# Modulation vectors and a column sum by fp32r matmuls, relu of phi(k) on ScalarE, and three moved groups of instructions, in a linear-attention and token-mixer block

## The chip, the cores and the metric

The kernel runs on one core of one Trainium2 chip. The metric is the time of one execution in device microseconds, lower is better. Three runs of the kernel before the change gave a median of 456.86 us.

## The reference

The input x has 2048 tokens of 448 channels. A conditioning vector c gives six modulation vectors of 448 numbers each. Two residual blocks follow: linear attention with 16 heads of 28 channels, and an MLP that mixes along the token axis with 1792 hidden units. All is float32.

```python
mod = silu(c) @ w_mod                       # (1,448) @ (448, 6*448): sa, ca, ga, sb, cb, gb
h = layernorm(x) * (1 + ca) + sa
q, k, v = heads(h @ wqkv)
phi = lambda t: where(t > 0, t + 1, exp(t)) + 1e-6
kv, z = phi(k)^T v, sum over tokens of phi(k)          # per head
o = (phi(q) kv) / (phi(q) z + 1e-6)
x = x + ga * (o @ wo)
h = layernorm(layernorm(x) * (1 + cb) + sb)
x = x + gb * ((gelu(h^T w1 + b1)) w2 + b2)^T
```

## The kernel before

**Numbers in two parts.** Most products run as fp32r matmuls. A float32 tile is cut into a high part (a ScalarE copy with an fp32r output) and a low part (VectorE subtracts the high part from the whole); `split` does both, lines 74 and 75. A product then takes three matmuls: high by high, high by low, low by high. A few matmuls are plain fp32; the trace shows each of those as two matmul instructions.

**Order.** The order on every engine is the order of the calls in the source: the scheduler is in its manual mode. Buffers come from pools. A tile of the pool `slots` (76 buffers) waits until the last readers of the buffer that it is given are done, so a new tile in the middle changes which buffer each later tile is given, and so what its writer waits for. PSUM has 8 banks.

**Stage one (up to 124 us).** x comes in 16 tiles of 128 tokens. For tile t VectorE makes the moments (`a_stats`, with a power on GpSimd, line 272) and the modulated norm (`a_norm_a`, `a_norm_b`, lines 277 and 283); ScalarE copies 64 columns of h once more (`a_dup`, line 287); TensorE transposes h (line 295); `a_split` cuts the transpose; `project` (11 matmuls, line 316) makes k. phi(k) is made by `a_exp` (line 323: exp on ScalarE) and `phi_k` (line 327: min with 1 and plus 1e-6 on VectorE; line 328: max of k in PSUM with 0, plus the former). `a_pk_parts` cuts phi(k): high part on ScalarE, low part either on VectorE (tiles in `DVE_LOW`) or by ScalarE's negated copy and an accumulating DMA that GpSimd issues (lines 357 and 358). A second accumulating DMA adds phi(k) to one of two running sums (line 383). `a_outer` (line 398, 11 matmuls) adds the outer product of phi(k) and h three steps later. The loop over t at line 514 takes these in an interleaved order; q of most tiles is left for later (`late`).

After the loop the running sums are summed over the tokens by two fp32 matmuls with a matrix of ones (`zp`, lines 574 to 576), `a_outer` of tile 15 follows, and the result is copied to `zb`. The outer products go through the value weights (`kvb`, line 598), a head mask, and wo (`wp`, line 723).

**Modulation vectors.** For vector j, four tiles of w_mod (112 by 448) are scaled by silu(c) and added on VectorE: `mod_acc` at one place (lines 156, 158) or `mod_part` one tile at a time (lines 164, 166). `mod_sum` (line 173) sums over the partitions by an fp32 matmul with ones, `mod_out` copies to SBUF. Vectors 1 and 0 are made at the very start, 2 inside the loop, 4 and 3 after it, 5 in stage two.

**Stage two (124 to 216 us).** A loop over i (line 731) takes, per round, the transposes of the normalized phi(q) (`tq`, line 642), the product with wo (`op`, line 658), a q projection while any is left, and from the fifth round the first MLP matmuls (`up`, lines 709 to 711) of tile i-5. VectorE's list per round is written out at lines 756 to 789; in it `b_recip`, `b_low2` (line 706, the low part of the normed tile, which waits for ScalarE's high part) and `b_scale` (line 631, `pn`, which the next round's `tq` reads) stand in this order.

**Stage three (216 us to the end)** is the rest of the MLP: w1 and w2 come in pieces, are cut and multiplied; part of the products of w2 use a scheme with seven products of halves.

Of the kernel before, what the change touches and what calls it, by code (L numbers as in the profile page):

```python
# [14 lines left out]
P = 128  # L15
# [3 lines left out]
G = 112  # L19
# [8 lines left out]
DVE_LOW = (0, 1, 13, 14, 15)  # L28
AHEAD = 8
LAG = 5  # L30
QS = {0: 2, 4: 2}
WARM = 12
WARM2, WARM3 = 10, 5
# [9 lines left out]
def block_kernel(ctx: ExitStack, tc: tile.TileContext, x, wqkv, wo, w1, b1, w2, b2, c, wmod, out):  # L43
# [16 lines left out]
    def slot(name, w=D, dt=F32, parts=P):  # L60
        return slots.tile([parts, w], dt, name=name, tag="slot", padded_shape=[P, 512])
# [5 lines left out]
    def moving(new, name, dt=F32R, parts=P):  # L67
        return new(name, dt=dt, parts=parts, w=512)[:, 16:16 + D]

    def bank(name):  # L70
        return psum.tile([P, 512], F32, name=name, tag="bank")
# [5 lines left out]

    ones = cst.tile([P, P], F32, name="ones")
    nc.vector.memset(ones, 1.0)
    ident = cst.tile([P, P], F32, name="ident")  # L80
    make_identity(nc, ident)
    mask = cst.tile([G, D], F32, name="mask")
# [78 lines left out]
    def mod_part(j, k):  # L161
        if k == 0:
            macc[j] = (tslot if j == 5 else slot)(f"acc{j}", parts=G)
            nc.vector.tensor_scalar_mul(macc[j], wm[j, 0], sc[:, 0:1])
        else:
            nc.vector.scalar_tensor_tensor(macc[j], wm[j, k], sc[:, k:k + 1], macc[j], op0=ALU.mult, op1=ALU.add)

    def mod_sum(j, n=4):
        ps = bank(f"modp{j}")
        todo = [(scb[:, (k - 2) * P:(k - 1) * P], wm[j, k]) for k in range(n, 4)]  # L170
        todo.insert(1, (ones[:G, :], macc.pop(j)))
        for k, (a, b) in enumerate(todo):
            nc.tensor.matmul(ps[:, :D], a, b, start=(k == 0), stop=(k == len(todo) - 1))
        return ps

    Whi, Wlo = {}, {}
# [13 lines left out]
    def w_low_dma(j, ch):  # L190
        w, r = Whi[j, ch], raw_w[j, ch]
        if ch < 3:
            Wlo[j, ch] = moving(tslot, f"wl{j}_{ch}")
            lo, hi = Wlo[j, ch], w
        else:
            lo = hi = w[64:128]
            r = r[64:128]
        nc.scalar.activation(lo, hi.bitcast(F32), AF.Copy, scale=-1.0)
        nc.gpsimd.dma_start(lo, r, accum_op=ALU.add)
# [119 lines left out]
    eks = {}  # L319

    def a_exp(t, ps):
        eks[t] = slot(f"ek{t}")
        nc.scalar.activation(eks[t], ps, AF.Exp)

    def phi_k(t, ps, new):
        dst, e = new(f"pk{t}"), eks.pop(t)
        nc.vector.tensor_scalar(e, e, 1.0, 1e-6, op0=ALU.min, op1=ALU.add)
        nc.vector.scalar_tensor_tensor(dst, ps, 0.0, e, op0=ALU.max, op1=ALU.add)
        return dst

    def phi_q(ps, name):
# [21 lines left out]
    def low(t, lo, full, hi):  # L353
        if t in DVE_LOW:
            nc.vector.tensor_sub(lo, full, hi.bitcast(F32))
        else:
            nc.scalar.activation(lo, hi.bitcast(F32), AF.Copy, scale=-1.0)
            nc.gpsimd.dma_start(lo, full, accum_op=ALU.add)
# [14 lines left out]
    def a_pk_parts(t):  # L373
        pk = pkf.pop(t)
        hi, lo = moving(slot, f"pkh{t}"), moving(slot, f"pkl{t}")
        nc.scalar.activation(hi, pk, AF.Copy)
        low(t, lo, pk, hi)
        if t in (0, 1, NT - 1):
            pksum.append(pk)
        elif t == NT - 2:  # L380
            pksum14.append(pk)
        else:
            nc.gpsimd.dma_start(pksum[t % 2], pk, accum_op=ALU.add)
        pks[t] = (hi, lo)
# [4 lines left out]
    def a_outer(t):  # L389
        if not cacc:  # L390
            cacc.extend(bank(f"cacc{ch}") for ch in range(4))
        xh, xl = xss.pop(t)
        kh, kl = pks.pop(t)
        for ch in range(4):
            s = slice(ch * P, (ch + 1) * P)
            todo = [(xh, kh), (xh, kl)] + ([(xl, kh)] if ch < 3 else [])
            for i, (a, b) in enumerate(todo):
                nc.tensor.matmul(cacc[ch][:, :D], a[:, s], b, start=(t == 0 and i == 0),  # L398
                                 stop=(t == NT - 1 and i == len(todo) - 1))
# [73 lines left out]
    a_exp(0, kp0)  # L473
    w_low_dma(0, 0)
    a_norm_b(2)
    w_low_dma(0, 1)
    a_stats(3)
    a_dup(2)
    a_pk(0, kp0)
# [34 lines left out]
    for t in range(3, NT):  # L514
        kp = project(t, 1, "kp")
        if t + 1 < NT:
            a_transpose(t + 1)
        a_outer(t - KV_LAG)
        if t in Q_EARLY:
            a_q(t)  # L520
        if t == 10:
            mp = mod_sum(2)
        if t + 1 < NT:
            a_split(t + 1)
        if t + 2 < NT:
            a_norm_a(t + 2)
        a_exp(t, kp)
        if t + 2 < NT:
            a_norm_b(t + 2)
        a_pk(t, kp)  # L530
        a_phi_q()
        a_pk_parts(t - 1)
        if t + 3 < NT:
            a_stats(t + 3)
        if t + 2 < NT:
            a_dup(t + 2)
        if t == 3:
            a_high(4)
        if t + 2 < NT:
            a_high(t + 2)  # L540
        if t == 10:
            mod_out(2, mp)
        if t + 4 < NT:
            load_x(t + 4)
        if 5 <= t < 9:
            mod_part(2, t - 5)
        if t in (10, 11):
            load_mod(14 - t)
        if t == 4:
            for g in range(4):  # L550
                w = tslot(f"wo{g}", parts=G)
                nc.sync.dma_start(w, wo[g * G:(g + 1) * G, :])
                wo_sb.append(w)
            load_qkv(2, tslot)
            b1c = cst.tile([P, NF], F32, name="b1c")
            nc.sync.dma_start(b1c, b1.rearrange("(k p) -> p k", p=P))
            b2c = cst.tile([P, NT], F32, name="b2c")
            nc.sync.dma_start(b2c, b2.rearrange("(k p) -> p k", p=P))
        if 11 <= t < 15:
            nc.vector.tensor_mul(wo_sb[t - 11], wo_sb[t - 11], mods[2][:G])  # L560
        load_to(PRE_LOAD.get(t, 0))
# [4 lines left out]
    a_phi_q()  # L566
    a_outer(NT - 3)
    a_outer(NT - 2)
    split_to(2)
    nc.vector.tensor_add(pksum[2], pksum[2], pksum14[0])  # L570
    nc.vector.tensor_add(pksum[2], pksum[2], pksum[1])
    a_q(late.pop(0))
    mod_acc(4)
    zp = bank("zp")
    for i, pk in enumerate((pksum[0], pksum[2])):
        nc.tensor.matmul(zp[:, :D], ones, pk, start=(i == 0), stop=(i == 1))
    a_outer(NT - 1)
    load_to(14)
    split_to(4)
    zb = tslot("zb")  # L580
    nc.scalar.activation(zb, zp[:, :D], AF.Copy)
    csum = []
    for ch in range(4):
        csum.append(slot(f"cs{ch}"))
# [4 lines left out]
    a_phi_q()  # L589
    a_q(late.pop(0))  # L590
    split_to(6)
    mp = mod_sum(4)
    mod_acc(3)
    kvb = bank("kvb")
    for ch in range(4):
        for g in range(4):
# [4 lines left out]
    kvm = slot("kvm", parts=G)  # L601
    nc.vector.tensor_mul(kvm, kvb[:G, :D], mask)
    mod_out(4, mp)
    mp = mod_sum(3)
    load_to(PRE + MID + 3)
    split_to(8)
    Wph, Wpl = [], []
# [18 lines left out]
    def b_recip(t):  # L626
        nc.vector.reciprocal(dens[t], dens[t])
# [103 lines left out]
    for i in range(NT + LAG):  # L731
        if i == NT - 4:
            load_mod(5)
        if NT - 3 <= i <= NT:
            mod_part(5, i - NT + 3)
        if i < NT:
            b_transpose(i)
        if 0 <= i - 1 < NT:
            b_out(i - 1)
        nq = min(len(late), QS.get(i, 1))  # L740
        for _ in range(nq):
            a_q(late.pop(0))
        t = i - LAG
        mp = mod_sum(5) if i == NT else None
        if t >= 0:
            if t == 0:
                accs = [bank(f"up{f}") for f in range(4)]
            if i > NT:
                if not early:
                    early = [bank(f"up{W1G[1][0] + f}") for f in range(W1G[1][1])]  # L750
                r = i - NT - 1
                step(NT + r, early, H2h[r], H2l[r], r == 0, False)
            step(t, accs, H2h[t], H2l[t], t == 0, t == NT - 1)
        if mp is not None:
            mod_out(5, mp)
        if i < NT:
            b_high(i)
        scale, res, norm1, norm2 = i + 1 < NT, 0 <= i - 2 < NT, 0 <= i - 3 < NT, 0 <= i - 4 < NT
        if res:
            b_res(i - 2)  # L760
        if scale:
            b_prod(i + 1)
        if norm2:
            b_norm2(i - 4, i)
        if res:
            b_mean1(i - 2, i)
        if norm1:
            b_norm1_a(i - 3)
        if scale:
            b_sum(i + 1)  # L770
        if norm1:
            b_norm1_b(i - 3, i)
        if scale:
            b_eps(i + 1)
        if i < NT:
            b_low(i)
        if norm1:
            b_mean2(i - 3, i)
        if scale:
            b_recip(i + 1)  # L780
        if norm2:
            b_low2(i - 4)
        if scale:
            b_scale(i + 1)
        a_phi_q(nq)
        load_to(14 + (i + 1) // 2)
        split_to(10 + (i + 1) // 2)
        if res or norm1:
            b_rstd(i, 0 if res else 1, 2 if norm1 else 1)
# [277 lines left out]
```

## Time and profile before

| | us |
|---|---|
| median of three runs (456.37 to 457.12) | 456.86 |
| the profiled execution | 457.06 |
| its span, first to last instruction | 455.3 |
| TensorE busy in the span | 448.9 |
| VectorE busy | 356.6 |
| ScalarE busy | 241.7 |
| GpSimd busy | 91.6 |

The profiled execution took 457.06 us, of which 455.3 lie between its first and its last instruction; 1.76 us lie around it. TensorE is granted its full clock throughout. A busy time of matmuls overlaps itself, since they are pipelined, so the cost of a matmul is read from the start of one to the start of the next.

### The profile page before, as it was taken

How to read it: one execution, taken by the hardware profiler on the slowest of the kernel's cores; microseconds unless marked ns; L12 is line 12 of the kernel's file. 1: busy time of each engine (PE TensorE's matmuls, PEld its weight loads, DVE VectorE, ACT ScalarE, POOL GpSimd, SP SyncE). 2: the span in 40 equal slices, each digit the busy share in tenths (PEclk: the TensorE clock that was granted, in tenths of full speed). 3: DMA queues.
4: the chain of work that ended last, by engine and by line, in shares of the span. 5: the costliest groups of instructions: out<-in, count | busy, mean ns of one | idle time of the engine just before them, and what ended most of it. 6: DMA issues, size and time to landing. Idle time of an engine off the chain costs nothing.

```text
span 455.3 us, 7265 instructions
## 1 busy us (share of the span) xinstructions
PE 448.9 (99%) x2378; PEld 409.9 (90%) x2378; DVE 356.6 (78%) x781; ACT 241.7 (53%) x538; POOL 91.6 (20%) x163
## 2 busy tenths in 40 slices
PE   8999999999999999999999999999999999999996
PEld 7589998988799999988999999999999999999995
DVE  4798897887899798896559676639696977798982
ACT  1649766644466576676675445236546262535350
POOL 2124676620014355554300000000000000000000
PEclk9999999999999999999999999999999999999999
DMA  7979999994200003322307553317960583528312
GB/s 220 283 186 168 170 175 225 229 219 141 71 1 2 23 24 88 74 50 48 116 22 228 171 187 113 115 40 235 281 185 23 186 231 120 170 96 254 112 57 97
DMA packets 60550, 61.85 MB, mean 136 GB/s; under 512 B 9248, under 2 KB 53856, under 8 KB 60512
## 3 DMA queue, kind: packets, MB, share of 16 engines
q1 hardware_dynamic: 54752, 52.45, 38.5%
q0 software_dynamic: 5760, 8.95, 12.0%
q8 instruction: 18, 0.29, 0.3%
q14 instruction: 20, 0.16, 0.1%
HBM read 45.09 MB, written 7.34 MB: 115 GB/s over the span
## 4 chain that ended last, share of the span: by engine, by line
PE 80%; POOL 4%; ACT 4%; DVE 4%; DMA 3%; issue 3%; SPq 1%; POOLq 0%; DVEq 0%
PE y L894 11%; PE up L711 8%; PE up L710 8%; PE up L709 8%; PE qp L316 7%; PE y L895 6%; PE cacc L398 5%; PE kp L316 5%; PE yp L709 4%; PE yp L711 4%; PE yp L710 4%; PE op L658 4%; DMA pkl<-pk 2%; DMA wm<-in_w_mod_dram 1%; ACT y L700 1%
## 5 line engine op out<-in xcount | busy, mean ns | idle before, releaser
L711 PE MATMUL up<-h2h,pl 128*128 128x448 f32 x224 | 81.3, 363 | 0.0
L710 PE MATMUL up<-h2l,ph 128*128 128x448 f32 x224 | 81.2, 362 | 0.0
L709 PE MATMUL up<-h2h,ph 128*128 128x448 f32 x224 | 81.1, 362 | 0.0
L75 DVE TENSOR_TENSOR pl<-pr,ph 128x512 fp32r<-128x512 f32 (+1 forms) x60 | 36.4, 616 | 12.3 <-ACT ph L74 7.9
L710 PEld LDWEIGHTS up<-h2l,ph 128*128 128x128 f32 x224 | 42.1, 188 | 3.3 <-issue 0.2
L709 PEld LDWEIGHTS up<-h2h,ph 128*128 128x128 f32 x224 | 41.9, 187 | 3.1 <-issue 0.2
L711 PEld LDWEIGHTS up<-h2h,pl 128*128 128x128 f32 x224 | 42.0, 188 | 2.4
L74 ACT ACTIVATE ph<-pr 128x512 fp32r<-128x512 f32 (+1 forms) x60 | 32.8, 567 | 15.9 <-PE up L710 11.1
L900 ACT ACTIVATE cc<-y 128x448 f32<-128x448 f32 x15 | 8.2, 546 | 55.4 <-PE y L895 38.6
L709 PE MATMUL yp<-uw,qw 128*128 128x448 f32 x84 | 31.2, 371 | 0.0
L710 PE MATMUL yp<-uw,qw 128*128 128x448 f32 x84 | 30.6, 365 | 0.0
L711 PE MATMUL yp<-uw,qw 128*128 128x448 f32 x84 | 30.6, 365 | 0.0
L398 PE MATMUL cacc<-pkh,xh 128*128 128x448 f32 x64 | 24.6, 385 | 0.0
L658 PE MATMUL op<-wph,pth 112*128 112x448 f32 x64 | 24.5, 383 | 0.0
L74 ACT ACTIVATE qw<-q 128x256 fp32r<-128x256 f32 (+1 forms) x56 | 18.9, 353 | 9.0 <-DMA q<-in_B_w_dram 8.5
L398 PE MATMUL cacc<-pkl,xh 128*128 128x448 f32 x64 | 23.3, 363 | 0.2 <-DMA pkl<-pk 0.2
L658 PE MATMUL op<-wph,ptl 112*128 112x448 f32 x64 | 23.2, 362 | 0.0
L658 PE MATMUL op<-wpl,pth 112*128 112x448 f32 x64 | 23.2, 362 | 0.0
L316 PE MATMUL kp<-wh,hh 128*128 128x448 f32 x60 | 22.0, 371 | 0.0
L316 PE MATMUL qp<-wh,hh 128*128 128x448 f32 x60 | 21.9, 371 | 0.0
L75 DVE TENSOR_TENSOR qw<-q,qw 128x256 fp32r<-128x256 f32 (+1 forms) x56 | 18.9, 352 | 3.8 <-ACT qw L74 3.8
L316 PE MATMUL kp<-wh,hl 128*128 128x448 f32 x60 | 21.7, 366 | 0.1
(198 smaller groups left out, 1221.0 us busy)
## 6 DMA issues: line engine op xcount, KB each, us to landing
pr<-in_B_w_dram SPq DMA_DIRECT2D x48, 256.0 KB, 3.0
a<-in_B_w_dram SPq DMA_DIRECT2D x20, 256.0 KB, 5.0
wm<-in_w_mod_dram SPq DMA_DIRECT2D x24, 196.0 KB, 5.0
a<-in_B_w_dram SPq DMA_DIRECT2D x20, 192.0 KB, 4.9
x<-in_A_x_dram SPq DMA_DIRECT2D x16, 224.0 KB, 4.6
xpark<-x SPq DMA_DIRECT2D x16, 224.0 KB, 1.9
q<-in_B_w_dram SPq DMA_DIRECT2D x28, 128.0 KB, 3.3
xb<-xpark SPq DMA_DIRECT2D x16, 224.0 KB, 4.1
```

Source lines behind the costliest of these rows:

```text
L74: nc.scalar.activation(hi, full, AF.Copy)
L75: nc.vector.tensor_sub(lo, full, hi.bitcast(F32))
L316: nc.tensor.matmul(o, a[:, ch * P:(ch + 1) * P], b, start=(n == 0), stop=(n == 10))
L398: nc.tensor.matmul(cacc[ch][:, :D], a[:, s], b, start=(t == 0 and i == 0), stop=(t == NT - 1 and i == len(todo) - 1))
L658: nc.tensor.matmul(opb[t][:, :D], a[:, s], b, start=(n == 0), stop=(n == 11))
L700: nc.scalar.activation(ys[t], ys[t], AF.Identity, bias=nb, scale=rs)
L709: nc.tensor.matmul(ps[:, :D], hi[:, sl], mh, start=first, stop=False)
L710: nc.tensor.matmul(ps[:, :D], hi[:, sl], ml, start=False, stop=False)
L711: nc.tensor.matmul(ps[:, :D], lo[:, sl], mh, start=False, stop=last)
L894: nc.tensor.matmul(ps[:, :D], h[:, s], w, start=opens and r == 0, stop=False, skip_group_check=True)
L895: nc.tensor.matmul(ps[:, :HD], l[:, s], w[:, :HD], start=False, stop=closes and r == PAIRS - 1, skip_group_check=True)
L900: nc.scalar.activation(cop[q, name], acc2[q, k][:, :D], AF.Copy)
```

## The change

1. A copy of the ones in fp32r, `ones_r`, is made on ScalarE at the start.
2. Modulation vectors 2, 3, 4 and 5: the accumulated tile is cut (`mod_split`: one ScalarE copy, one VectorE subtraction) and summed by two fp32r matmuls (`mod_sum2`) instead of one fp32 matmul. Vectors 1 and 0 stay.
3. The sum of phi(k): VectorE adds the second running sum to the first, the result is cut, and two fp32r matmuls replace two fp32 ones; they stand behind `a_outer` of tile 15 instead of ahead of it. The share of 1e-6 comes in as a bias of 2048 times 1e-6 in the copy to `zb`.
4. phi(k): ScalarE makes relu(k) beside exp(k), and VectorE takes one instruction instead of two. The 1e-6 moves into the bias of the high part's copy and into the low part's instruction.
5. The scaled additions for vectors 4 and 3 leave their two blocks of four behind the loop; they stand in steps 11 to 15 of the loop and just behind it.
6. The low part of one q weight tile moves from ScalarE and an accumulating DMA to VectorE.
7. In stage two `b_scale` stands ahead of `b_low2`.

```diff
+MOD_AT = {11: [(4, 0)], 12: [(4, 1)], 13: [(4, 2)], 14: [(4, 3)], 15: [(3, 0), (3, 1)]}
...
+    ones_r = cst.tile([P, P], F32R, name="ones_r")
+    nc.scalar.activation(ones_r, ones, AF.Copy)
...
+    def mod_split(j):
+        acc = macc.pop(j)
+        macc[j] = (moving(slot, f"mh{j}", parts=G), moving(slot, f"ml{j}", parts=G))
+        split(acc, *macc[j])
+
+    def mod_sum2(j):
+        ps = bank(f"modp{j}")
+        hi, lo = macc.pop(j)
+        nc.tensor.matmul(ps[:, :D], ones_r[:G, :], hi, start=True, stop=False)
+        nc.tensor.matmul(ps[:, :D], ones_r[:G, :], lo, start=False, stop=True)
+        return ps
...
     def a_exp(t, ps):
-        eks[t] = slot(f"ek{t}")
-        nc.scalar.activation(eks[t], ps, AF.Exp)
+        eks[t] = (slot(f"ek{t}"), slot(f"rk{t}"))
+        nc.scalar.activation(eks[t][0], ps, AF.Exp)
+        nc.scalar.activation(eks[t][1], ps, AF.Relu)
     def phi_k(t, ps, new):
-        dst, e = new(f"pk{t}"), eks.pop(t)
-        nc.vector.tensor_scalar(e, e, 1.0, 1e-6, op0=ALU.min, op1=ALU.add)
-        nc.vector.scalar_tensor_tensor(dst, ps, 0.0, e, op0=ALU.max, op1=ALU.add)
+        dst, (e, r) = new(f"pk{t}"), eks.pop(t)
+        nc.vector.scalar_tensor_tensor(dst, e, 1.0, r, op0=ALU.min, op1=ALU.add)
...
-        nc.scalar.activation(hi, pk, AF.Copy)
-        low(t, lo, pk, hi)
+        nc.scalar.activation(hi, pk, AF.Copy, bias=1e-6)
+        if t in DVE_LOW:
+            nc.vector.scalar_tensor_tensor(lo, pk, 1e-6, hi.bitcast(F32), op0=ALU.add, op1=ALU.subtract)
+        else:
+            nc.scalar.activation(lo, hi.bitcast(F32), AF.Copy, scale=-1.0, bias=1e-6)
+            nc.gpsimd.dma_start(lo, pk, accum_op=ALU.add)
...
-    w_low_dma(0, 1)
+    w_low(0, 1)
...
         if t == 10:
-            mp = mod_sum(2)
+            mp = mod_sum2(2)
...
+        if t == 9:
+            mod_split(2)
+        for j, i in MOD_AT.get(t, ()):
+            mod_part(j, i)
...
     a_outer(NT - 2)
+    for i in (2, 3):
+        mod_part(3, i)
     split_to(2)
...
-    mod_acc(4)
+    nc.vector.tensor_add(pksum[2], pksum[2], pksum[0])
+    zs = (moving(slot, "zh"), moving(slot, "zl"))
+    split(pksum[2], *zs)
+    a_outer(NT - 1)
     zp = bank("zp")
-    for i, pk in enumerate((pksum[0], pksum[2])):
-        nc.tensor.matmul(zp[:, :D], ones, pk, start=(i == 0), stop=(i == 1))
-    a_outer(NT - 1)
+    for i, pk in enumerate(zs):
+        nc.tensor.matmul(zp[:, :D], ones_r, pk, start=(i == 0), stop=(i == 1))
+    mod_split(4)
+    mod_split(3)
...
-    nc.scalar.activation(zb, zp[:, :D], AF.Copy)
+    nc.scalar.activation(zb, zp[:, :D], AF.Copy, bias=S * 1e-6)
...
-    mp = mod_sum(4)
-    mod_acc(3)
+    mp = mod_sum2(4)
...
-    mp = mod_sum(3)
+    mp = mod_sum2(3)
...
+        if i == NT:
+            mod_split(5)
...
-        mp = mod_sum(5) if i == NT else None
+        mp = mod_sum2(5) if i == NT else None
...
+        if scale:
+            b_scale(i + 1)
         if norm2:
             b_low2(i - 4)
-        if scale:
-            b_scale(i + 1)
```

## The prediction

> **What bounds the kernel now.** I read the page's first part, then TensorE's waits, then the chain that ended last.
>
> ```profile
> span 455.3 us, 7265 instructions
> PE 448.9 (99%) x2378; PEld 409.9 (90%) x2378; DVE 356.6 (78%) x781; ACT 241.7 (53%) x538; POOL 91.6 (20%) x163
> ```
>
> Busy matmuls overlap, so 99% alone proves little. The waits of TensorE do (who for whom; total, times, longest): behind the first 15 us one row holds nearly all that there is,
>
> ```profile
> PE tq L642 <- DVE pn L631: 0.6, 2, 0.4
> ```
>
> So TensorE's own work sets the time, and each microsecond taken from it counts, unless another chain is level with it at that place. Where that is so, the chain that ended last tells (start, length, what):
>
> ```profile
> 66.58 7.55 DMA pkl<-pk
> ...
> 91.69 0.61 DVE hl L75
> ...
> 108.07 1.50 PE zp L576 x4
> 109.57 2.21 PE cacc L398 x11
> 111.79 2.21 PE qp L316 x11
> 113.99 0.75 PE modp L173 x2
> 114.75 3.15 PE kvb L598 x32
> ...
> 214.64 0.75 PE modp L173 x2
> ```
>
> Twice it leaves TensorE: from 64 to 92 us through GpSimd and its DMAs, and from 159 to 207 us through ScalarE, VectorE and GpSimd. From 92 to 159 and from 207 on it is TensorE. The table by stretches (length, then busy time of PE, weight loads, DVE, ACT, POOL; clock, DMA share, GB/s) says why:
>
> ```profile
> 38.00:44.00 6.00, 6.00 (x33) 5.39 (x32) 5.10 (x12) 5.74 (x14) 3.26 (x5) 1.00 0.93 163
> 62.00:93.00 31.00, 30.61 (x160) 27.59 (x160) 25.80 (x61) 19.35 (x41) 19.60 (x24) 1.00 1.05 219
> 164.00:216.00 52.00, 51.39 (x270) 46.99 (x268) 44.98 (x105) 35.04 (x74) 27.23 (x59) 1.00 0.26 62
> ```
>
> From 62 to 93 us the DMA engines are full (share 1.05) beside TensorE; in stage two VectorE is at 86% (44.98 of 52.00) and TensorE has 0.61 idle.
>
> **The change part by part.** *The sums on TensorE.* An fp32 sum is two instructions: `modp` takes 0.75 twice in the chain (vectors 4 and 5; I take it for vector 3 too), `zp` with two sums 1.50. An fp32r matmul of 448 columns takes 2.21/11 = 0.20 (the `cacc` row). After the change each vector has two of these, 0.40, and the sum of phi(k) too. Gains: `zp` 1.50 - 0.40 = 1.10; vectors 4, 3, 5: 3 x 0.35 = 1.05. Vector 2 would give 0.35 as well, but it stands near 76 us, where the chain isn't TensorE's: I count nothing.
>
> *Their parts.* Each cut adds a ScalarE copy and a VectorE subtraction of about 0.6, five times. `zp` must find `zl` ready. It now stands behind `cacc` of tile 15, at 110.28 by the old clock (108.07 + 2.21). Ahead of `zl` VectorE has, counted from 106.0, where the old block for vector 4 begins, what was put in earlier for vector 3 (four instructions), the third addition and `zl` itself.
>
> ```profile
> 103.36 0.69 DVE L75 TENSOR_TENSOR pl<-pr,ph 128x512 fp32r<-128x512 f32 x1 [1.08 <-PE cacc L398]
> ...
> 106.02 0.45 DVE L156 TENSOR_SCALAR acc<-wm,sc 112x448 f32<-112x448 f32 x1
> 106.51 2.12 DVE L158 SCALAR_TENSOR_TENSOR acc<-wm,sc,acc 112x448 f32<-112x448 f32 x3
> ```
>
> Vector 3's four cost 0.45 + 2.12 = 2.57, as vector 4's do here; the wait of 1.08 and an `ek` of 0.39 go, so 1.1 stays: 106.0 + 1.1 + 0.6 for the addition, 0.6 for ScalarE's `zh`, 0.6 for `zl` make 108.9, 1.4 before it is wanted. If that cover were gone, the delay would count in full, from 110.28 on. `ml4` and `ml3` follow by 110.4, wanted at about 113; the copies to `zb` and of `cacc` end by 112.4 on ScalarE, `kvb` wants the first at 113.3. VectorE loses the second block of four there, so `kvm` stays behind `kvb` only. `ml5` waits for ScalarE, whose queue is busy until 212.3 (`pl` below, 211.69 + 0.63), so it ends at 213.6 against 214.5 at which `modp` 5 is wanted; behind it on VectorE waits the residual of tile 14, whose followers wait for GpSimd until 214.8 in any case.
>
> ```profile
> 211.69 0.63 ACT L226 ACTIVATE pl<-ph 128x512 fp32r<-128x512 f32 x1
> ```
>
> *phi(k).* By groups (busy, mean ns, idle before and whom for):
>
> ```profile
> L327 DVE TENSOR_SCALAR ek<-ek 128x448 f32<-128x448 f32 x16 | 6.2, 386 | 1.5 <-ACT ek L323 1.5
> L335 DVE SCALAR_TENSOR_TENSOR pq<-eq,rq 128x448 f32<-128x448 f32 x16 | 9.9, 622 | 4.7 <-ACT rq L334 4.7
> L334 ACT ACTIVATE rq<-qp 128x448 f32<-128x448 f32 x16 | 8.7, 541 | 0.0
> L287 ACT ACTIVATE h<-h 128x64 f32<-128x64 f32 x15 | 3.8, 254 | 16.7 <-DVE h L283 16.7
> ```
>
> VectorE loses 0.39 per tile, and its remaining instruction takes `pq`'s form, 0.62. ScalarE gains 0.54 per tile. It is covered: before the copy L287 ScalarE idles 16.7 us over 15 tiles, 1.1 per tile. The exception is 38 to 44 us (5.74 of 6.00 busy), where the relu may hold `a_dup`'s copy and the transposes behind it by 0 to 0.54; the chain's stretch to 92.34 takes that up, so 0. Here a rule of the Trainium skill speaks against the edit: "ScalarE: Activation LUTs", Rules for kernel authors, wants relu on VectorE and not on ScalarE. This trace agrees on the engine time (541 against 386 ns). By the rule, 16 tiles times 0.155 us would be lost, 2.5 us, an estimate from rows; by the idle time above nothing is.
>
> *What is queued behind the relu*: `pkh`, `pkl` and so GpSimd's accumulating DMA, whose landing TensorE awaits: the first row of the chain lands at 66.58 + 7.55 = 74.13, and the matmul below starts at 74.18, 0.69 after its forerunner instead of 0.20. The delay is up to 0.54. Against it stands the landing itself: 7.55 us, where the group's median is 4.2.
>
> ```profile
> 73.49 0.45 PE L398 MATMUL cacc<-pkh,xh 128*128 128x448 f32 x1
> 74.18 0.47 PE L398 MATMUL cacc<-pkl,xh 128*128 128x448 f32 x1 [0.24 <-DMA pkl<-pk]
> ```
>
> ```profile
> pkl<-pk POOLq DMA_DIRECT2D x11, 224.0 KB, 4.2
> ```
>
> In the built order the loads that ran beside it (x of tile 14, w_mod of vector 4) and two w1 pieces wait for later owners of their buffers, since each step takes one tile more; the first q weight's accumulating DMA is gone. So the landing may be up to 3.3 earlier too. I take 0, and -0.8 to +1.2 as ends: this wait of 0.49 and the one of 0.31 at 92 us (below) gone, or three DMAs each later by 0.4.
>
> *Additions for vectors 4 and 3 in the loop.* The matmul at 92.34 starts 0.51 after the one before instead of 0.20, waiting for `hl`:
>
> ```profile
> 91.83 0.37 PE L316 MATMUL kp<-wl,hh 128*128 128x448 f32 x1
> 92.34 0.47 PE L316 MATMUL kp<-wh,hl 128*128 128x448 f32 x1
> ...
> 195.09 0.37 PE L711 MATMUL up<-h2h,pl 128*128 128x448 f32 x1
> 195.84 0.62 PE L642 MATMUL tq<-ident,pn 128*112 128x128 f32 x4 [0.38 <-DVE pn L631]
> ...
> 206.19 0.37 PE L711 MATMUL up<-h2h,pl 128*128 128x448 f32 x1
> 206.78 0.62 PE L642 MATMUL tq<-ident,pn 128*112 128x128 f32 x4 [0.23 <-DVE pn L631]
> ```
>
> In step 11 VectorE gains a scaling and loses an `ek`, level; in step 12 it gains 0.6 and loses 0.4 ahead of this `hl`: +0.15. TensorE coming earlier only waits longer here, which is why vector 2's 0.35 is lost. For the additions in steps 13 to 15 I count nothing: from 92 on the chain is TensorE's, so VectorE is ahead there.
>
> *`pn` ahead of `h2l`.* TensorE starts `tq` 0.75 and 0.59 after its forerunner instead of 0.20: 0.55 + 0.39 = 0.94 lost, both times for `pn`. VectorE's list there:
>
> ```profile
> 194.53 0.62 DVE L706 TENSOR_TENSOR h2l<-y,h2h 128x448 fp32r<-128x448 f32 x1 [0.19 <-ACT h2h L703]
> 195.08 0.62 DVE L631 SCALAR_TENSOR_TENSOR pn<-pq,den 128x448 f32<-128x448 f32 x1
> ```
>
> `pn` stands behind `h2l`, which itself waits 0.19 for ScalarE. In front it ends 0.55 + 0.19 = 0.74 earlier: both stalls go, 0.94. `h2l` is later by 0.6 at most, and is read a round later (about 5.5, half of 206.78 - 195.84). Next late is the power on GpSimd that the norm waits for, which does not touch `tq`.
>
> The q weight's part on VectorE (+0.6, -0.4 at that place) and `ones_r` (ScalarE's wait for c hides it) I cost at nothing; without cover each is under 0.3.
>
> Sum: -1.10 - 1.05 - 0.94 + 0.15 = -2.94. The profiled execution took 457.06 (1.76 around its span); 454.1. It stands 0.2 above the median of 456.86, so I forecast **453.9**.
>
> **Rivals.** *(a) The relu makes ScalarE the bound: slower.* From tile 3 to 15 each step grows by 0.54: 13 x 0.54 = 7.0, and 453.9 + 7.0 = 460.9. For it speak the 38 to 44 row and the accumulating DMAs behind ScalarE; against it 19.35 of 31.00 busy from 62 to 93. It decides once ScalarE's idle time per step, 1.1, falls under 0.54. The Trainium skill's rule above is on this side. Chance 0.06.
>
> *(b) Stage two gives it back: no change.* The chain from 159 to 207 isn't TensorE's. If it starts from its own place, the 1.65 us gained before 124 (1.10 + 0.70 - 0.15) end in `tq` waiting for `pn`; left are vector 5's 0.35 and what VectorE itself gains, its wait of 0.19 for `h2h` in two rounds: 456.86 - 0.73 = 456.1. For: VectorE 44.98 of 52. Against: VectorE itself waits for TensorE's q products there (4.7 for `rq`), so its start moves along. Chance 0.15.
>
> *(c) The DMAs of 62 to 93 us get shorter*, and vector 2's 0.35 and the waits come back: 453.9 - 0.8 - 0.15 = 452.9. Chance 0.12.
>
> *(d) The two stalls stay*, since TensorE arrives earlier and `pn` is late again: 453.9 + 0.94 = 454.8. Chance 0.09.
>
> **How the numbers follow.** The forecast has 0.58, with 453.1 to 455.1 by the ends of the DMA term. With (c) and (d) that is 0.79, so the range reaches on to (b): 452.8 to 456.2. About 0.2% (0.9 us) is what a measurement of this kernel can tell from no change. Faster by more: 0.58 + 0.12 + 0.09 = 0.79; (b) lies within: 0.15; slower: 0.06.
>
> **What would show it.** Right: `modp` and `zp` pairs at 0.40 from start to start; no TensorE wait for `pn`; `kp` still waiting for `hl` near 92; ScalarE's idle before L287 down to about 0.6 per tile. Wrong: TensorE waits for `pkl`'s landing or for the copy L287 in several steps (a), or `tq` waiting in every round from 160 on (b), or `zp` waiting for `zl`.

## The result, and the profile after

The changed kernel took 454.0 us (median of six, 453.72 to 454.72) against 456.99 us (456.28 to 457.24) for the kernel before. The ratio is 0.9932, with a 95% interval of 0.9915 to 0.9950. The forecast was 453.9. The profiled execution took 453.73 us; its span is 3.3 us shorter than the one before.

The page's first part, after:

```profile
span 452.0 us, 7271 instructions
PE 445.9 (99%) x2376; PEld 409.7 (91%) x2376; DVE 355.2 (79%) x772; ACT 250.1 (55%) x559; POOL 88.4 (20%) x162
```

ScalarE has 8.4 us more, VectorE 1.4 less, TensorE 3.0 less. All that TensorE waits for (who for whom; total, times, longest):

```profile
PE warm L140 <- DVE mhalf L94: 1.1, 1, 1.1
PE kp L332 <- DVE hl L76: 0.8, 1, 0.8
PE tp L436 <- DVE h L431: 0.2, 1, 0.2
PE modp L176 <- DMA wm<-in_w_mod_dram: 0.2, 1, 0.2
```

The row of `tq` for `pn` is gone, and the one of `cacc` for the landing of `pkl` too. In their place is one wait of 0.8 for `hl`. In the chain that ended last (start, length, what) the sums now read:

```profile
109.81 0.40 PE zp L606 x2
110.21 2.20 PE qp L332 x11
112.41 0.21 PE modp L188
112.62 0.20 PE modp L189
```

`zp` went from 1.50 to 0.40, `modp` from 0.75 to 0.41. The table by stretches, same columns as before:

```profile
38.00:44.00 6.00, 6.00 (x33) 5.59 (x33) 4.80 (x11) 5.86 (x14) 2.94 (x5) 1.00 1.08 165
62.00:93.00 31.00, 30.21 (x162) 27.59 (x161) 25.48 (x57) 22.31 (x48) 19.22 (x25) 1.00 1.05 217
164.00:216.00 52.00, 51.91 (x274) 48.05 (x273) 45.56 (x105) 35.90 (x77) 26.00 (x59) 1.00 0.26 62
```

In stage two TensorE's idle time fell from 0.61 to 0.09. From 62 to 93 us it rose from 0.39 to 0.79. TensorE's own list shows both places:

```profile
90.72 0.37 PE L332 MATMUL kp<-wl,hh 128*128 128x448 f32 x1
91.88 0.47 PE L332 MATMUL kp<-wh,hl 128*128 128x448 f32 x1 [0.79 <-DVE hl L76]
...
203.33 0.37 PE L741 MATMUL up<-h2h,pl 128*128 128x448 f32 x1
203.79 0.62 PE L672 MATMUL tq<-ident,pn 128*112 128x128 f32 x4
```

The first pair is 1.16 apart instead of 0.20, so 0.96 is lost to `hl` of tile 14, where 0.31 was lost before. The second is 0.46 apart: 0.26 is left of the 0.94 for `pn`.

The balance of the two profiles, from start to start: `zp` -1.10; vectors 4, 3 and 5 about -1.05; vector 2 -0.35; `pn` -0.68; the landing of `pkl` -0.49; `hl` of tile 14 +0.65; the first 42 us -0.37, of which 0.23 is a load at the very start (6.38 instead of 6.61). The sum is -3.4, against 3.3 between the spans. The head of a profile, its first 25 us, varies without the change: the projection whose first matmul starts at 25.25 before and at 25.01 after starts between 24.43 and 25.25 in the profiles of this document, so absolute times of two profiles are compared only to some tenths.

### The profile page after: what moved, and what is told of

The parts are those of the page before. It is cut to its first block, busy times and chain, and to the rows that moved or that the text cites. A ratio compares the mean times of both kernels' runs of the same rounds, so it can differ in the third digit from the quotient of the medians.

```text
span 452.0 us, 7271 instructions
## 1 busy us (share of the span) xinstructions
PE 445.9 (99%) x2376; PEld 409.7 (91%) x2376; DVE 355.2 (79%) x772; ACT 250.1 (55%) x559; POOL 88.4 (20%) x162
## 3 DMA queue, kind: packets, MB, share of 16 engines
HBM read 45.09 MB, written 7.34 MB: 116 GB/s over the span
## 4 chain that ended last, share of the span: by engine, by line
PE 86%; POOL 4%; issue 4%; DMA 2%; DVE 1%; SPq 1%; ACT 1%; POOLq 0%; DVEq 0%
PE y L926 11%; PE up L741 10%; PE up L740 10%; PE up L739 10%; PE op L688 9%; PE qp L332 7%; PE y L927 6%; PE yp L739 4%; PE yp L741 4%; PE yp L740 4%; PE cacc L419 3%; PE kp L332 3%; PE tq L672 2%; POOL xl L375 1%; DMA wm<-in_w_mod_dram 1%
```

## The experiments

Each kernel was timed beside the kernel before, in three sets of four; the kernel before took 456.58, 457.17 and 456.79 (medians of 23, 17 and 17 runs, 455.83 to 459.35 in all). The line numbers are each kernel's own.

### First set: the base, and three parts undone

**after_again** is the changed kernel once more.

> The changed kernel once more, as the base for the others of this set. 454.0, ratio to before 0.9935. In its profile the only TensorE waits behind 20 us are the one for hl of tile 14 (0.96 over the usual step) and one for pn near 203 us (0.26). If the early landing of pkl of tile 7 was chance, the old wait of 0.49 near 73 us comes back here.

It took 453.44 (452.86 to 454.18), ratio 0.9930 (0.9915 to 0.9945). The profile has the wait for `hl` (0.90) and the one for `pn` (0.26), and none for `pkl`.

**no_relu**

```diff
-        nc.scalar.activation(eks[t][1], ps, AF.Relu)
...
-        nc.vector.scalar_tensor_tensor(dst, e, 1.0, r, op0=ALU.min, op1=ALU.add)
+        nc.vector.tensor_scalar(e, e, 1.0, 1e-6, op0=ALU.min, op1=ALU.add)
+        nc.vector.scalar_tensor_tensor(dst, ps, 0.0, e, op0=ALU.max, op1=ALU.add)
...
```

The 1e-6 and the biases go back with it.

> The changed kernel with part 4 undone: phi(k) by two VectorE instructions as before, no relu on ScalarE; the relu's buffer is still taken, unused, so that the buffers' order stays. Theory of the prediction (ScalarE's idle time covers the relu; VectorE has 0.39 more per tile): the only place where it shows is hl of tile 14, whose wait grows from 0.96 by 0.1 to 0.5; 454.1 to 454.5. Rival (relu on the slower engine costs 0.155 per tile on the path): 2.5 shorter, 451.5. Rival (the relu delays the accumulating DMAs): the wait for hl of tile 14 shrinks, 453.5.

It took 455.78 (453.95 to 456.31), ratio 0.9973 (0.9960 to 0.9985): 2.3 more than the base, far outside what any of the three theories expected (the two profiles, single runs, differ by 1.7 in their spans). Two of the rows of what its TensorE waits for, and then the place of the longest of the new waits:

```profile
PE cacc L419 <- DMA pkl<-pk: 0.9, 1, 0.9
PE kp L332 <- DVE hl L76: 0.6, 1, 0.6
```

```profile
83.96 0.45 PE L419 MATMUL cacc<-pkh,xh 128*128 128x448 f32 x1
85.28 0.47 PE L419 MATMUL cacc<-pkl,xh 128*128 128x448 f32 x1 [0.87 <-DMA pkl<-pk]
```

1.11 over the usual step is lost to the landing of `pkl` of tile 9, and 0.28 to that of tile 7; the wait for `hl` of tile 14 is 0.75, smaller than the base's. Two early `hl`, near 25 and 40 us, cost 0.22 each, which the base does not lose:

```profile
25.07 0.37 PE L332 MATMUL kp<-wl,hh 128*128 128x448 f32 x1
25.49 0.47 PE L332 MATMUL kp<-wh,hl 128*128 128x448 f32 x1
```

In the base's profile, with the relu on ScalarE, neither the waits for landings nor the two early ones for `hl` are there.

**swap_back**

```diff
-        if scale:
-            b_scale(i + 1)
         if norm2:
             b_low2(i - 4)
+        if scale:
+            b_scale(i + 1)
```

> The changed kernel with part 7 undone: the low part of the normed tile ahead of pn again. Theory: the two waits of tq for pn come back, 0.94 in place of the 0.26 that is left: +0.7, 454.7. Rival (the waits went for another reason, or come back in each round, since TensorE arrives 2.5 earlier than before): no change, 454.0, or one wait per round from 160 us on, over 456.

It took 454.12 (453.70 to 454.54), ratio 0.9945 (0.9929 to 0.9961): 0.68 more than the base by the medians, though the two intervals overlap. The profile agrees: the row is back,

```profile
PE tq L672 <- DVE pn L661: 0.6, 2, 0.3
```

and the two steps are 0.50 and 0.39 too long, 0.89 in all against the base's 0.26. TensorE's earlier arrival did not bring further waits, so the rival is out.

**zp_fp32**

```diff
-    nc.vector.tensor_add(pksum[2], pksum[2], pksum[0])
-    zs = (moving(slot, "zh"), moving(slot, "zl"))
-    split(pksum[2], *zs)
+    zs = (pksum[0], pksum[2])
...
-        nc.tensor.matmul(zp[:, :D], ones_r, pk, start=(i == 0), stop=(i == 1))
+        nc.tensor.matmul(zp[:, :D], ones, pk, start=(i == 0), stop=(i == 1))
```

> The changed kernel with the sum of phi(k) by two plain fp32 matmuls of the two running sums again (no third addition, no cut), at the new place behind the outer product of tile 15. Theory: +1.10 on TensorE, nothing else: 455.1, ratio 0.9959. Rival (what follows waits for kvm or the cuts anyway): +0.4 or less, 454.4.

It took 454.61 (453.58 to 456.71), ratio 0.9959 (0.9943 to 0.9975): 1.17 more than the base by the medians, as the theory had it, with intervals that just overlap; in its chain `zp` takes 1.50 again. Its runs spread over 3 us, and its profile, taken in a run of 456.20, shows one reason:

```profile
82.72 0.45 PE L419 MATMUL cacc<-pkh,xh 128*128 128x448 f32 x1
84.82 0.47 PE L419 MATMUL cacc<-pkl,xh 128*128 128x448 f32 x1 [1.66 <-DMA pkl<-pk]
```

The edit acts behind 104 us and leaves the order up to there as the changed kernel has it, whose two profiles have no such wait. So the landing of `pkl` varies by over a microsecond between executions of what is, up to there, one order of instructions, and a wait for it in a single profile is a sample.

### Second set: what the relu does, and what holds hl of tile 14

**no_relu_no_sums** is no_relu without the running sums' DMAs.

```diff
-        else:
-            nc.gpsimd.dma_start(pksum[t % 2], pk, accum_op=ALU.add)
```

> The kernel of no_relu, which was 2.3 slower than the changed one (455.78 against 453.44) where at most 0.5 was expected, and whose profile has TensorE waiting for the landing of pkl at 73.5 and 84.0 us (0.28 and 1.11). Here the twelve accumulating DMAs of the running sums of phi(k) are left out, so the sum of phi(k) is not the reference's; GpSimd's queue has 23 accumulating DMAs in the place of 35. Theory Q (without the relu VectorE reaches the variance later, the power on GpSimd waits for it, and the DMAs queued behind it issue and land later): with the queue emptied the waits for pkl go, and the time falls to 453.5 to 454.4, the wait for hl of tile 14 staying or shrinking. Rival V (VectorE's own 0.39 per tile stands in TensorE's path): the time stays within 0.4 of 455.8.

It took 453.52 (452.87 to 453.94), ratio 0.9917 (0.9901 to 0.9933). The loss of no_relu is gone, and the long wait for `pkl` too: the rows of what TensorE waits for are only

```profile
PE warm L140 <- DVE mhalf L94: 1.1, 1, 1.1
PE modp L176 <- DMA wm<-in_w_mod_dram: 0.2, 1, 0.2
PE tp L434 <- DVE h L429: 0.2, 1, 0.2
```

From start to start it still loses 0.26 to `pkl` of tile 7, 0.22 at each of the two early `hl`, and 0.25 at `hl` of tile 14, where the base loses 0.90. So the 2.3 hang on the accumulating DMAs, and the time of rival V is out. VectorE's 0.39 does reach TensorE's path, at the two early `hl`, but those 0.44 are made up by the shorter wait at tile 14.

Theory Q's own mechanism is not borne out in full, however: in no_relu the power waits for VectorE hardly longer than in the changed kernel. The groups of GpSimd's powers between 40 and 93 us (busy, mean ns, idle before), no_relu first:

```profile
L288 POOL TENSOR_TENSOR rs<-ve,mhalf 128x1 f32<-128x1 f32 x10 | 9.4, 936 | 0.9 <-DVE ve L286 0.8 <-DVE xh L382 0.2
```

```profile
L288 POOL TENSOR_TENSOR rs<-ve,mhalf 128x1 f32<-128x1 f32 x10 | 10.0, 1004 | 0.6 <-DVE xh L382 0.6
```

What differs is how long the transfers take. The long wait is for `pkl` of tile 9, issued at the same time in both kernels (77.80 and 77.92). From the DMAs issued from 75.2 to 79 us (number, KB, us to landing), of no_relu and then of the changed kernel:

```profile
wm<-in_w_mod_dram SPq DMA_DIRECT2D x4, 196.0 KB, 4.9
pkl<-pk POOLq DMA_DIRECT2D x1, 224.0 KB, 7.4
```

```profile
wm<-in_w_mod_dram SPq DMA_DIRECT2D x3, 196.0 KB, 4.6
pkl<-pk POOLq DMA_DIRECT2D x1, 224.0 KB, 5.1
```

Four loads of w_mod go out beside the transfer of 7.4, three beside that of 5.1. That the loads are the cause is not shown: zp_fp32 has three there as well, and 7.0. In no_relu_no_sums four stand beside it, and it takes 6.1; it is issued 1.5 earlier (76.27) and lands in time. Leaving out the running sums takes twelve DMAs out of GpSimd's list and off the DMA engines at once, and no run held the loads apart with all else equal. So how much of the 2.3 is the load on the DMA engines, how much the order of the loads and how much GpSimd's queue stays open.

**relu_alone** is the kernel before with part 4 alone (the diff of part 4 above).

> The kernel before with part 4 alone (relu of phi(k) on ScalarE, the 1e-6 in the cuts, the bias in the copy to zb). The prediction's term: 0, with ends -0.8 and +1.2. Theory Q (the relu frees GpSimd's queue): the wait of 0.49 for pkl of tile 7 goes and part of the 0.31 for hl of tile 14, so 0.5 to 0.8 faster: 455.9, ratio 0.9985. Rival (the slower engine's 0.155 per tile): 2.5 slower, 459.1. Rival (all of no_relu's 2.3 belongs to the relu in any surroundings): 454.3.

It took 456.98 (456.16 to 458.13), ratio 0.9991 (0.9979 to 1.0003): no change that can be told, as the prediction's term had it. Neither the rival's loss of 2.5 nor a gain of 2.3 is seen. ScalarE's idle time before `a_dup` is down to 0.61 per tile (9.2 over 15), as forecast, and TensorE still waits for `pkl`:

```profile
L287 ACT ACTIVATE h<-h 128x64 f32<-128x64 f32 x15 | 3.8, 254 | 9.2 <-DVE h L283 9.2
```

```profile
PE cacc L402 <- DMA pkl<-pk: 1.1, 1, 1.1
```

**adds_late**

```diff
-MOD_AT = {11: [(4, 0)], 12: [(4, 1)], 13: [(4, 2)], 14: [(4, 3)], 15: [(3, 0), (3, 1)]}
+MOD_AT = {13: [(4, 0)], 14: [(4, 1), (4, 2)], 15: [(4, 3), (3, 0), (3, 1)]}
```

> The changed kernel with the scaled additions of vectors 4 and 3 in steps 13, 14 and 15 (none in 11 and 12, ahead of hl of tile 14). Theory L (VectorE's list decides when hl of tile 14 is cut: 0.45 and 0.60 go from ahead of it): the wait of 0.9 falls to 0 to 0.4, 452.5 to 453.0. Rival P (the norm of tile 14 waits for the power on GpSimd, which stands behind an accumulating DMA): hl ends at most 0.2 earlier, and the time stays at 453.4.

It took 453.14 (452.78 to 454.06), ratio 0.9912 (0.9896 to 0.9929). The wait for `hl` is gone; `hl` ends at 90.55 instead of 91.83, of which 0.33 is an earlier head of the profile. By the time it can't be told from the base (the intervals overlap): its profile has 0.67 for `pkl` of tile 9 at 82.93 instead, which also makes TensorE come later to `hl`. VectorE's list and what it waits for there:

```profile
86.65 0.69 DVE L299 SCALAR_TENSOR_TENSOR h<-h,rs,mod 128x448 f32<-128x448 f32 x1 [0.74 <-POOL rs L288]
...
89.33 0.62 DVE L585 TENSOR_TENSOR wo<-wo,mod 112x448 f32<-112x448 f32 x1
89.86 0.69 DVE L76 TENSOR_TENSOR hl<-tp,hh 128x512 fp32r<-128x512 f32 x1
```

Theory L holds for the most part: even with the head taken off, `hl` ends 0.95 earlier. The first row shows that P has its part as well: the norm waits 0.74 for the power.

**power_first**

```diff
-            nc.gpsimd.dma_start(pksum[t % 2], pk, accum_op=ALU.add)
+            add_later.append((pksum[t % 2], pk))
...
         if t + 3 < NT:
             a_stats(t + 3)
+        for dst, pk in add_later:
+            nc.gpsimd.dma_start(dst, pk, accum_op=ALU.add)
+        add_later.clear()
```

> The changed kernel with each running-sum DMA of GpSimd moved behind the power of the same step (line 288). Theory P: the 0.47 that the norm of tile 14 waits for the power goes, the wait for hl of tile 14 falls from 0.9 to about 0.45: 453.0. Theory L: VectorE's list fills the 0.47 at another place, nothing changes: 453.4. A cost is possible: the power waits for VectorE's variance, and each running-sum DMA now stands behind it, later by up to 1; if pkl lands later by that, TensorE waits, 454 or more.

It took 452.37 (median of four, 451.92 to 452.74), ratio 0.9893 (0.9874 to 0.9912): faster than both kernels, its interval lying just under the base's. It gained 1.1 on the base by the medians (1.7 by the ratios), more than theory P had. In the changed kernel GpSimd's list near 86 us was

```profile
85.26 0.86 POOL L404 DMA_DIRECT2D pk<-pk  x1 [1.06 <-issue]
85.82 1.11 POOL L288 TENSOR_TENSOR rs<-ve,mhalf 128x1 f32<-128x1 f32 x1
```

and in power_first it is

```profile
83.93 0.88 POOL L288 TENSOR_TENSOR rs<-ve,mhalf 128x1 f32<-128x1 f32 x1
85.22 0.89 POOL L559 DMA_DIRECT2D pk<-pk  x1 [0.40 <-issue]
```

The power ends 2.1 earlier (84.81 instead of 86.93; 0.36 of it is the head of the profile), since it no longer stands behind a DMA that GpSimd can't issue yet. `hl` of tile 14 ends at 90.16, and its matmul follows at the usual step (90.26, then 90.46):

```profile
90.26 0.36 PE L332 MATMUL kp<-wl,hh 128*128 128x448 f32 x1
90.46 0.36 PE L332 MATMUL kp<-wh,hl 128*128 128x448 f32 x1
```

### Third set: vector 2, and how far the better order carries

**vec2_fp32**

```diff
-            mp = mod_sum2(2)
+            mp = mod_sum(2)
...
-        if t == 9:
-            mod_split(2)
```

> The changed kernel with vector 2 summed by the plain fp32 matmul again (no cut of it). Theory of the prediction (TensorE is not the last there, so vector 2's 0.35 is worth nothing): the wait for hl of tile 14 shrinks from 0.9 to 0.55 and the time stays, ratio 0.993. Rival (it counts in full): +0.35, ratio 0.9938. VectorE also loses a subtraction of 0.6 in step 9, so pkl of tiles 8 to 10 may land earlier, which would show as nothing here, as TensorE does not wait for them.

It took 453.56 (453.26 to 454.82), ratio 0.9928 (0.9908 to 0.9947), beside the base's 0.9930: no change. The wait for `hl` shrank from 0.96 (0.90 in the second profile) to 0.58, by what the sum took longer:

```profile
90.58 0.37 PE L332 MATMUL kp<-wl,hh 128*128 128x448 f32 x1
91.36 0.47 PE L332 MATMUL kp<-wh,hl 128*128 128x448 f32 x1 [0.41 <-DVE hl L76]
```

So vector 2's 0.35 on TensorE is spent in waiting, as the prediction had it. Here the four loads of w_mod beside `pkl` of tile 7 go out together, as in the kernel before; the transfer takes 6.47, and TensorE does not wait for it.

**power_first_no_relu** has the edits of power_first and of no_relu.

> power_first (0.9893) with part 4 undone. Theory Q (the relu was worth 2.3 in the changed kernel, since it kept GpSimd's queue ahead): if the order of the running-sum DMAs alone does the same, the time is near power_first, 0.990; if the power's wait for VectorE's variance is what holds the queue, it stays in front of the xl and running-sum DMAs, and most of the 2.3 is lost again: 0.994 to 0.996, with TensorE waiting for pkl. Rival V (VectorE's 0.39 per tile in the path): 2.3 more than power_first in any order, 0.9943, without a wait for pkl.

It took 454.48 (453.90 to 455.33), ratio 0.9944 (0.9925 to 0.9963): most of the 2.3 is lost again, 2.1 by the medians, and TensorE waits for `pkl` twice. In this order the power's wait for VectorE does show. The powers between 40 and 93 us, here and in power_first:

```profile
L288 POOL TENSOR_TENSOR rs<-ve,mhalf 128x1 f32<-128x1 f32 x10 | 9.2, 916 | 5.6 <-DVE xh L382 3.4 <-DVE ve L286 2.1
```

```profile
L288 POOL TENSOR_TENSOR rs<-ve,mhalf 128x1 f32<-128x1 f32 x10 | 8.5, 849 | 1.7 <-DVE ve L286 1.0 <-DVE xh L382 0.5
```

**power_first_before** is the kernel before with the edit of power_first.

> The kernel before with only the running-sum DMAs moved behind the power. Theory Q: the waits of TensorE between 70 and 93 us (0.49 and 0.31 in its profile, more in slower runs) go: 0.5 to 1.0 faster, ratio 0.998 to 0.999. Rival (in the kernel before the queue is held by VectorE's variance and not by the running sums): no change, 1.000, or slower where the sums come later.

It took 456.97 (455.63 to 457.96), ratio 0.9997 (0.9983 to 1.0011): no change; its profile still has 0.40 for `pkl` of tile 7. The powers idle 4.8 there, waiting for VectorE, where they idle 0.4 in the kernel before without the edit. So the order brings nothing that can be told by itself. It does not seem to need the relu, however: on no_relu it brought 1.3 (454.48 against 455.78, in two sets; by the ratios, 0.9944 against 0.9973, the same, with intervals that just meet). Which other part of the change lets it pay, no run shows.

**power_first_vec5_late**

```diff
-        if NT - 3 <= i <= NT:
-            mod_part(5, i - NT + 3)
+        for n in {NT - 2: (0,), NT - 1: (1, 2), NT: (3,)}.get(i, ()):
+            mod_part(5, n)
```

> power_first with the four scaled additions of vector 5 at rounds 14 (one), 15 (two) and 16 (one) instead of one in each of 13 to 16, so that 0.45 and 0.23 of VectorE go from ahead of the last two pn. Theory (the wait of 0.26 for pn of tile 15 is VectorE's list): it goes, 452.1, ratio 0.9887. Rival (that pn waits through VectorE's norm for the power on GpSimd, 0.54 idle there): no change, 0.9893.

It took 452.92 (452.39 to 453.82), ratio 0.9911 (0.9890 to 0.9933). The wait for `pn` near 203 us went, but 0.44 for `pkl` of tile 7 stands in its profile, and the time can't be told from power_first, nor from the base. Whether it gains the 0.26 stays open; and as it holds the edit of power_first too, the gain of power_first rests on the four times of its own.

## Why the prediction was right

The total was met within 0.1: 453.9 forecast, 454.0 measured. Its terms were not all met; two errors went against each other, at `pn` and at `hl` of tile 14, so that it was met so closely is in part luck.

*The sums.* `zp` fell by 1.10 in the chain, as forecast, and undoing it cost 1.17. The vectors have 0.41 in the place of 0.75. Vector 2's 0.35 was counted at nothing; vec2_fp32 shows that this is so.

*Their parts.* `zl` had to be ready at 109.85 and was at 108.28, 1.57 ahead where 1.4 was forecast:

```profile
107.66 0.62 DVE L76 TENSOR_TENSOR zl<-pk,zh 128x448 fp32r<-128x448 f32 x1 [0.64 <-ACT zh L75]
```

No sum of a vector waits for its parts.

*pn ahead of h2l.* Forecast 0.94, measured 0.68. One of the two stalls went, 0.26 of the other stayed. The term set the 0.74 that `pn` gains against a TensorE that stands still. By the lists, that `pn` ends 3.0 earlier (203.64 against 206.65), of which 0.74 is the swap, and TensorE is ready for it 2.9 earlier: VectorE's list itself had gained less than TensorE. This is rival (d) in part, 0.26 of its 0.94.

*hl of tile 14.* By the forecast the matmul behind `hl` would start 0.15 later than before, at 92.49, whatever TensorE gains ahead of it. It started at 91.88, 0.46 earlier than before: this is the term that was mis-sized, by 0.61. About 0.24 of the 0.46 is the head of the profile, not the change. The wait itself grew by 0.65, since TensorE arrives 1.11 earlier (vector 2's 0.35 and the 0.49 of `pkl` among it) and `hl` ends only 0.47 earlier. The prediction had named vector 2's part as lost there. What holds `hl` is the additions ahead of it on VectorE (adds_late) and the power that stands behind an accumulating DMA (power_first). The prediction counted the additions, as its 0.15, but did not look at the power here; it named GpSimd's power as the next to be late only in stage two.

With these, the profiles' sum is -1.10 - 1.05 - 0.68 - 0.46 = -3.29, against -2.94 in the forecast and 3.3 between the spans.

*The DMAs of 62 to 93 us.* Taken at 0, with -0.8 as the end. The wait of 0.49 for `pkl` went, as the prediction's better end had it, but the time of rival (c) did not follow, since what was gained there was spent at `hl`. The transfer takes 5.6 instead of 7.55:

```profile
pkl<-pk POOLq DMA_DIRECT2D x1, 224.0 KB, 5.6
```

The reason that the prediction gave, loads that come later beside it, fits, as two of the four loads of w_mod come later here. It is not shown: in vec2_fp32 the four stand together, and the wait is gone too.

*phi(k).* The relu was taken as covered by ScalarE's idle time. That held: in the stretch from 38 to 44 us ScalarE is busy 5.86 of 6.00 and TensorE has no idle time at all, and ScalarE keeps 11.9 us of idle time ahead of `a_dup`'s 15 copies, so rival (a) fell. The relu takes 552 ns on ScalarE (row below), and no loss from it is seen. So the rule of the Trainium skill ("ScalarE: Activation LUTs", Rules for kernel authors) to use VectorE for relu, and the 2.5 us that the prediction estimated by it, are not borne out here: ScalarE's price is higher, but ScalarE had the time.

```profile
L340 ACT ACTIVATE rk<-kp 128x448 f32<-128x448 f32 x16 | 8.8, 552 | 0.0
```

What the prediction missed is that some of the other parts lean on it. It priced the q weight's low part, vector 2's cut and the additions at next to nothing and the relu at nothing, each against the kernel before. Each alone may be so (relu_alone: 0.9991), but without the relu the rest of the change brings 0.8 instead of 3.1 (456.58 - 455.78, against 456.58 - 453.44). Which part leans on it, no run shows.

*Rival (b)* fell: from 160 us on TensorE waits for `pn` once, 0.26, and vector 5's gain and the gains ahead of it arrive at the end.

## What to carry to other kernels

Price the parts of a change together wherever two chains are level: here TensorE and the string of GpSimd's accumulating DMAs were within half a microsecond, and a part worth nothing alone was worth 2.3 in company. When an engine arrives earlier, look for the next wait in every queue that feeds it, GpSimd's too, and not only on the engine whose list was edited. Try a small operation that others wait for (the power of a norm) ahead of a DMA issue in an engine's list: this brought 1.1 or more in the changed kernel and nothing that can be told in the kernel before.

## What the runs showed of the hardware

GpSimd's accumulating DMAs are issued at the pace at which earlier ones land. Its list in no_relu:

```profile
66.62 0.87 POOL L398 DMA_DIRECT2D pkl<-pk  x1 [0.65 <-ACT pkl L397]
68.76 0.86 POOL L404 DMA_DIRECT2D pk<-pk  x1 [1.27 <-DVE ve L286]
69.32 0.88 POOL L288 TENSOR_TENSOR rs<-ve,mhalf 128x1 f32<-128x1 f32 x1
71.28 0.89 POOL L375 DMA_DIRECT2D xl<-h  x1 [1.08 <-ACT pkl L397]
74.28 0.89 POOL L398 DMA_DIRECT2D pkl<-pk  x1 [2.11 <-PE tp L311]
```

The DMA issued at 66.62 landed after 7.34, at 73.96; the third one behind it was issued at 74.28, 0.3 later. The one of 74.28 landed after 3.2, at 77.48, and the third behind it was issued at 77.80. The same step of 0.3 behind the landing of the third before is found up to 86 us, so no more than three are under way here. In none of the kernels does GpSimd issue one less than 0.2 behind that landing. At 74.28 the profile names another engine as the releaser (`PE tp`); its last transpose before that ended at 73.78. Why it is three, no run shows.
